# A fused attention and mixer kernel: first pair in parts of two slots, five additive pairs, and a new rule for ScalarE's relus

## The chip, the core and the metric

The kernel runs on one core of a Trainium2 chip. The metric is the device time of one execution in microseconds (us), taken as the median of several runs. The core has TensorE (PE in the profile, with PEld for its weight loads), VectorE (DVE), ScalarE (ACT), GpSimd (POOL) and SyncE (SP), each with its own instruction queue that is worked off in order. [...] SP, ACT and POOL can also issue DMAs.

## What is computed

Four batches, eight heads, 768 positions, head dimension 64. Attention is block-sparse: block i of 32 positions sees itself, its neighbours, the first and the last block and three sampled blocks. An MLP-mixer layer follows, first over the tokens, then over the channels:

```python
mask = np.abs(blk_i - blk_j) <= window
mask = mask | (blk_i == 0) | (blk_j == 0) | (blk_i == n_blocks - 1) | (blk_j == n_blocks - 1)
for qb in range(n_blocks):
    for kb in sampled_blocks[qb]:
        mask[qb*block:(qb+1)*block, kb*block:(kb+1)*block] = True
scores = np.where(mask, scale * np.matmul(q, k.transpose(0, 1, 3, 2)), -1e9)
attn   = softmax(scores)
x      = (attn @ v), heads side by side               # (4, 768, 512)
h      = np.maximum(x^T @ w_tok1, 0.0) @ w_tok2
u      = x + h^T
out    = u + np.maximum(u @ w_ch1, 0.0) @ w_ch2
```

## The kernel before

Two heads make a pair; there are 16 pairs, four to a batch. A pair has nine steps: 3 blocks of 256 queries (t) times 3 blocks of 256 keys (jj). One step is four score matmuls into a PSUM tile `ps` (two such tiles exist), one `exp` of 128x1024 on ScalarE into `et`, and eight value matmuls (`po`). After three steps VectorE divides by the row sums and writes `x`. So a step has one exp and 12 matmuls.

The mask is applied in one of two ways. In the first `NT0` = 4 pairs it is additive: 24 more rows lie under the 64 rows of q and k (`R` = rows 64 to 87, one per block of 32), with an indicator of the key's block on the k side and the entries of `t2add` (0 or -30000) on the q side, so that the score matmul adds the mask itself. It then has 88 rows, and each head has its own buffer columns. From pair 4 on the two heads lie in rows 0 to 63 and 64 to 127, and VectorE multiplies each `et` by a 0/1 `mask` (L709). That mask is spread by GpSimd out of a small one while the first pairs run.

Keys and queries arrive with positions in rows and are turned on TensorE (pairs 1 to 7) or by the DMA's transpose (pairs 8 to 15). Additive pairs take the turn straight from the loaded tile and are evacuated one head at a time (L662); the others are laid out again on VectorE first (L570).

The mixer's work for batch 0 is done per pair in small pieces (`tok_first`: L913, L936, L945, L959, L971). Only when all four of these are done can `ch`, the channel part (L994 for `w_ch1`, L1020 for `w_ch2`), run in earnest. From there on `ch` fills TensorE between attention steps, since it needs no exp.

The order on every engine is written by `Planner`: a small clock with a price for each operation picks, whenever an engine is free, the ready operation of highest priority; streams are `qk_stream`, `pv_stream`, the turns, the token parts and `ch`. The planner's order is what the chip then works off; its prices only decide that order. A relu of `ch` may go to VectorE or ScalarE (`relu_op`, L819 and L821). ScalarE takes one only while no score tile waits for its exp (`exp_pending`).

The first pair is written by hand ahead of the planner. Its q and k come as fp32 in halves of three slots (a slot is 128 positions). ACT issues the first half of q, SP the sampled blocks, both halves of k, then the second half of q. They are cast (L392), turned (L400) and evacuated (L408). GpSimd makes the indicator `ind` with two `affine_select`s over 24x768 (L331, L335), then the identity (L339), and then issues the loads: v of pair 0, k, q and v of pairs 1 and 2, the token weights, pair 3 (L259, L267). VectorE makes `t2add` in fourteen small operations (L358 to L380). `e2_mm` (L415) multiplies `t2add` with the indicator to make the q-side rows for 384 queries, and `e2_copy` (L422) puts them into `qtb`. Meanwhile `idle_mm` (L321) keeps TensorE running. The planner starts at a set time `START`.

Of the kernel before, what the change touches and what calls it, by code (L numbers as in the profile page):

```python
# [10 lines left out]
I32 = mybir.dt.int32  # L11
# [39 lines left out]
class Planner:  # L51
# [8 lines left out]
    PE_LAT, SEM = 180.0, 50.0  # L60
    tight = 40e3
# [42 lines left out]
    def step(self):  # L104
# [31 lines left out]
        for eng in ("act", "dve", "sp"):  # L136
# [3 lines left out]
            best = None  # L140
            for o in self.ops:
                prio, num, engines, cost, deps, emit, done, lat, tags = o
                if eng not in engines:
                    continue
                if eng == "act" and prio > 0 and self.exp_pending:
                    continue
                t = self.when(deps, tags)
                if t is None:
                    continue
                if t <= self.now:  # L150
                    if best is None or (prio, num) < best[:2]:
                        best = o
                else:
                    nxt.append(t)
# [20 lines left out]
def kernel(  # L175
# [24 lines left out]
    NT0 = 4  # L200
    TOKP = 0.7
# [23 lines left out]
    dma = {"free": 7.95 * US, "n": 0}  # L225
    RATE = 200.0
    LATE = (0, 290, 350, 0, 0, 190, 40, 700, 0)
# [8 lines left out]
    def flat(ap):  # L236
# [4 lines left out]
        for n in range(NR)  # L241
# [3 lines left out]
    homes[4]["v"] = flat(ktb[0][:, 1, :])  # L245
    homes.append({"k": flat(qtb[0][:, 1, :]), "q": flat(ktb[1][:, 1, :]), "v": flat(qtb[1][:, 1, :])})
    homes.append({"k": flat(ktb[2][:, 1, :]), "q": flat(qtb[2][:, 1, :]), "v": flat(ktb[3][:, 1, :])})
# [4 lines left out]
                  "v": flat(half["q"][:, 0:S])})  # L252

# [51 lines left out]
    first(nc.sync, "k", k, 1)  # L305
# [3 lines left out]
    ind = ktb[0][:, 0, :].rearrange("k (c p) -> k c p", c=NC)  # L309
    kbi = sb1.tile([128, 24], I32, name="kbi")  # L310
# [9 lines left out]
    def idle_mm():  # L320
        nc.tensor.matmul(  # L321
            out=idle_ps[:, 0, :], lhsT=free(one[:, 0:1], 0, [[0, 128]]),
            rhs=free(one[:, 0:1], 0, [[0, 512]]), start=True, stop=True,
        )

    for i in range(8):
        idle_mm()
# [4 lines left out]
        out=ind[R, :, :], in_=free(one[R, 0:1], 0, [[0, NC], [0, 128]]), compare_op=ALU.is_ge,  # L332
        fill=0.0, base=0, pattern=[[1, NC], [NC, 128]], channel_multiplier=-32,
    )
    nc.gpsimd.affine_select(  # L335
        out=ind[R, :, :], in_=ind[R, :, :], compare_op=ALU.is_ge, fill=0.0,
        base=31, pattern=[[-1, NC], [-NC, 128]], channel_multiplier=32,
    )
    nc.gpsimd.affine_select(  # L339
# [3 lines left out]
    load_pair(0, 3.4 * US, 0, ("v",))  # L343
    load_pair(1, 4.2 * US, 1)
# [5 lines left out]
    sampf = sb1.tile([128, 6], FP32, name="sampf")  # L350
    kbf = sb1.tile([128, 24], FP32, name="kbf")
    dkf = sb1.tile([128, 24], FP32, name="dkf")
    edge = sb1.tile([128, 1], FP32, name="edge")
    bandg = sb1.tile([128, 24], FP32, name="bandg")
    allow = sb1.tile([128, 24], FP32, name="allow")
    t2add = sb1.tile([128, 24], BF16, name="t2add")

    nc.vector.tensor_copy(out=dkf[R, :], in_=dki[R, :])  # L358
    nc.vector.tensor_copy(out=edge[R, :], in_=qbi[R, :])
    nc.vector.tensor_tensor(out=dkf[R, :], in0=dkf[R, :], in1=dkf[R, :], op=ALU.mult)  # L360
    nc.vector.tensor_scalar(
        out=edge[R, :], in0=edge[R, :], scalar1=-11.5, scalar2=None, op0=ALU.add
    )
    nc.vector.tensor_tensor(out=edge[R, :], in0=edge[R, :], in1=edge[R, :], op=ALU.mult)
    nc.vector.tensor_scalar(
        out=edge[R, :], in0=edge[R, :], scalar1=121.0, scalar2=None, op0=ALU.is_gt
    )
    nc.vector.tensor_scalar(
        out=bandg[R, :], in0=dkf[R, :], scalar1=1.0, scalar2=edge[R, 0:1],
        op0=ALU.is_le, op1=ALU.max,  # L370
    )
    nc.vector.memset(free(bandg[R, 0:1], 0, [[23, 2]]), 1.0)
    nc.vector.tensor_copy(out=kbf[R, :], in_=kbi[R, :])
    nc.vector.tensor_copy(out=sampf[R, :], in_=samp64[R, :].bitcast(I32))
    for col, other in ((0, bandg), (2, allow), (4, allow)):
        nc.vector.scalar_tensor_tensor(
            out=allow[R, :], in0=kbf[R, :], scalar=sampf[R, col : col + 1], in1=other[R, :],
            op0=ALU.is_equal, op1=ALU.max,
        )
    nc.vector.tensor_scalar(  # L380
        out=t2add[R, :], in0=allow[R, :], scalar1=-MASKVAL, scalar2=MASKVAL,
        op0=ALU.mult, op1=ALU.add,
    )
    indf = ind[R, :, :].rearrange("k c p -> k (c p)")
    nc.vector.tensor_copy(out=ktb[0][R, 1, 0:384], in_=indf[:, 0:384])
    bandrows = free(ind[R, 0, :], 0, [[0, 2], [1, S]])
    for n in range(1, NV):
        nc.sync.dma_start(out=ktb[n][R, :, :], in_=bandrows)


    def first_lay(copy, nm, hf):
        copy(  # L392
            out=lay0[nm][:, 3 * hf : 3 * hf + 3, :, :],
            in_=f32[nm][:, :, 3 * hf : 3 * hf + 3, :].rearrange("p h c d -> p c h d"),
        )

    def first_turn(nm, hf):
        t = psM.tile([128, 3, 128], BF16, tag="pm", name=f"t{nm}first{hf}")
        for c in range(3):
            nc.tensor.matmul(  # L400
                out=t[:, c, :], lhsT=lay0[nm][:, 3 * hf + c, :, :].rearrange("p h d -> p (h d)"),
                rhs=ident[:, :], start=(c == 0), stop=(c == 2), is_transpose=True,
            )
        return t

    def first_evac(copy, nm, hf, hd, t):
        buf = (ktb if nm == "k" else qtb)[0]
        copy(  # L408
            out=buf[0:64, hd, 384 * hf : 384 * hf + 384],
# [3 lines left out]
    def e2_mm(hf, pool, tag):  # L413
        t = pool.tile([128, 512], FP32, tag=tag, name=f"pm_e2_{hf}")
        nc.tensor.matmul(  # L415
            out=t[R, 0:384], lhsT=t2add[R, :], rhs=indf[:, 384 * hf : 384 * hf + 384],
            start=True, stop=True,
        )
        return t

    def e2_copy(copy, hf, hd, t):
        copy(out=qtb[0][R, hd, 384 * hf : 384 * hf + 384], in_=t[R, 0:384])  # L422

    vcopy, acopy = nc.vector.tensor_copy, nc.scalar.copy
    first_lay(acopy, "q", 0)
    qt0 = first_turn("q", 0)
    first_lay(acopy, "k", 0)
    kt0 = first_turn("k", 0)
    e2a, e2b = e2_mm(0, psM, "pm"), e2_mm(0, psO, "po")
    for i in range(4):  # L430
        idle_mm()
    first_evac(acopy, "q", 0, 0, qt0)
    first_evac(acopy, "q", 0, 1, qt0)
    e2_copy(acopy, 0, 0, e2a)
    first_evac(vcopy, "k", 0, 0, kt0)
    first_evac(vcopy, "k", 0, 1, kt0)
    e2_copy(vcopy, 0, 1, e2b)
    first_lay(acopy, "k", 1)
    first_lay(vcopy, "q", 1)
    START = 6.3 * US  # L440
# [3 lines left out]
    P.free_at["dve"] = START + 550.0  # L444
    f_there = {("k", 0): Ev(START), ("q", 0): Ev(START), ("k", 1): Ev(), ("q", 1): Ev()}

# [4 lines left out]
    def first_rest():  # L451

        def band(eng):
            nc.vector.tensor_copy(out=ktb[0][R, 1, 384:S], in_=indf[:, 384:S])

        P.op(("dve",), {"dve": 250.0}, [], band, prio=0)
        for nm in ("k", "q"):
            box, last, rel = {}, Ev(), Ev()

            def emit(nm=nm, box=box, rel=rel):  # L460
                P.take("pm", rel)
                box["t"] = first_turn(nm, 1)

            yield 330.0, [Ev(START + (200.0 if nm == "k" else 600.0))], [("pm", 1)], emit, last
            for hd in range(2):
                def evac(eng, nm=nm, hd=hd, box=box):
                    first_evac(vcopy, nm, 1, hd, box["t"])

                ev = P.op(("dve",), {"dve": 350.0}, [last], evac, prio=0)
                f_there[nm, 1].same_as = ev  # L470
                rel.same_as = ev
        box, last, rel = {}, Ev(), Ev()

        def emit():
            P.take("pm", rel)
            box["t"] = e2_mm(1, psM, "pm")

        yield 330.0, [], [("pm", 1)], emit, last
        for hd in range(2):
            def copy(eng, hd=hd, box=box):  # L480
                e2_copy(vcopy, 1, hd, box["t"])

            e2_there = P.op(("dve",), {"dve": 555.0}, [last], copy, prio=0)
            rel.same_as = e2_there
        rows_there[0] = e2_there
        built.add(("row", 0))
        for n in range(1, NV):
            def spread(eng, n=n):
# [6 lines left out]
                ("dve",) if n == 1 else ("sp",), {"dve": 560.0, "sp": 800.0}, [e2_there], spread,  # L495
# [104 lines left out]
    def transposes(p):  # L600
# [4 lines left out]
        if p == 0:  # L605
# [3 lines left out]
            for hd in range(2):  # L609
                kT_there[p, hd], qT_there[p, hd] = f_there["k", 1], f_there["q", 1]  # L610
# [108 lines left out]
    def qk_deps(p, t, jj):  # L719
# [3 lines left out]
        deps = [f_there["k", int(jj > 0)], f_there["q", int(t > 0)]]  # L723
        return deps + [rows_there[0]] * (t > 0)

    def qk_stream():
        todo = list(steps)
        while todo:
# [13 lines left out]
            s2 = todo.pop(0)  # L742
            yield lambda p=s2[0]: (p, 1) in qT_there
            evs = [Ev(), Ev()], [Ev(), Ev()]

            def emit(s=s, s2=s2, evs=evs):
                scores(s, evs[0][0], evs[1][0])
                scores(s2, evs[0][1], evs[1][1])
# [410 lines left out]
```

## Time and profile before

| | us |
|---|---|
| median of 9 runs | 255.72 |
| lowest, highest | 255.0, 258.23 |
| the profiled execution | 255.03 |
| its span in the trace | 253.3 |
| PE busy in the span | 245.3 |
| DVE busy | 179.5 |
| ACT busy, of it 144 exps | 174.4, of it 139.1 |

Two of the nine runs lie at 258; the other seven between 255.0 and 255.81. The profiled execution is 1.7 us longer than its span. A row of instructions in the profile gives line, engine, operation, output<-input, shapes and count, then busy time and the mean duration of one in ns, then the engine's idle time before them and what ended it. A timeline row gives start, duration, the same names, and in brackets the idle time before it. A matmul's duration includes its pipeline's latency, so the distance between starts, not the duration, is what it costs TensorE.

### The profile page before, as it was taken

The page shows a single profiled execution, that of the slowest core. Times are in us where ns is not written, and L with a number is a line of the kernel's source. Part 1 is how long each engine was busy: PE and PEld are TensorE (multiplying, and loading weights), DVE is VectorE, ACT ScalarE, POOL GpSimd, SP SyncE. Part 2 cuts the span into 40 slices and gives each one's busy share as a digit, 9 for nine tenths or more (in the row PEclk, how much of TensorE's full clock was granted, in tenths as well). Part 3 has the DMA queues.
Part 4 walks back from the last instruction along what each step waited for, and adds up shares of the span by engine and source line. Part 5 has one row for each costly group of instructions (what it writes and reads, how often), then busy time and mean ns, then how long its engine had stood idle before and what let it go on. Part 6 is the DMA issues. An engine that isn't in the chain of part 4 may idle for free.

```text
span 253.3 us, 6660 instructions
## 1 busy us (share of the span) xinstructions
PE 245.3 (97%) x2786; PEld 159.7 (63%) x2805; DVE 179.5 (71%) x394; ACT 174.4 (69%) x216; POOL 49.9 (20%) x84
## 2 busy tenths in 40 slices
PE   8889999999999999999999999999999999999995
PEld 3679999756666456656676566567567644566444
DVE  7884878998898988899889898978985312200222
ACT  5899999888888577778888777677786510277000
POOL 8846979477300000000000000000000000000000
PEclk9999999999999999999999999999999999999999
DMA  5999999999955935254032212311400212300132
GB/s 145 191 215 202 211 203 205 204 201 201 201 89 126 155 90 95 40 136 103 3 77 51 62 44 46 102 44 44 104 3 1 55 51 84 124 3 0 41 115 94
DMA packets 42462, 26.36 MB, mean 104 GB/s; under 512 B 23680, under 2 KB 38800, under 8 KB 42432
## 3 DMA queue, kind: packets, MB, share of 16 engines
q0 software_dynamic: 15104, 12.98, 32.3%
q1 hardware_dynamic: 27056, 12.76, 20.5%
q8 instruction: 22, 0.36, 0.6%
q10 hardware_dynamic: 272, 0.20, 0.3%
q14 instruction: 8, 0.07, 0.1%
HBM read 26.74 MB, written 6.29 MB: 130 GB/s over the span
## 4 chain that ended last, share of the span: by engine, by line
PE 90%; ACT 4%; DVE 3%; issue 1%
PE pm_ch L994 25%; PE pm_ch L1020 24%; PE ps L691 16%; PE po L777 14%; ACT et L701 3%; PE pm_tok L882 3%; PE pm_tok L857 3%; PE ps_idle L321 2%; PE pm_tok L913 1%; DVE et L709 1%; PE pm_tok L936 1%; PE tk L633 1%; DVE qtb L422 0%; DVE qtb L662 0%; PE tq L633 0%
## 5 line engine op out<-in xcount | busy, mean ns | idle before, releaser
L701 ACT ACTIVATE et<-ps 128x1024 bf16<-128x1024 f32 x144 | 139.1, 1022 | 31.8 <-PE ps L691 30.9
L994 PE MATMUL pm_ch<-uT,w_ch 128*128 128x384 bf16 x384 | 72.6, 326 | 0.1
L709 DVE TENSOR_TENSOR et<-et,mask 128x1024 bf16<-128x1024 bf16 x108 | 70.3, 682 | 1.2 <-ACT et L701 1.2
L1020 PE MATMUL pm_ch<-w_ch,rc 128*128 128x512 bf16 (+2 forms) x293 | 67.8, 362 | 1.1 <-issue 0.3
L777 PEld LDWEIGHTS <-et 128*128 128x128 bf16 x1152 | 47.6, 97 | 16.6 <-issue 3.4
L691 PE MATMUL ps<-qtb,ktb 64*128 64x256 bf16 (+1 forms) x576 | 54.6, 272 | 2.4 <-ACT et L701 2.1
L777 PE MATMUL po<-vaug,et 128*128 128x65 bf16 x1152 | 54.3, 193 | 0.3 <-DVE et L709 0.2
L994 PEld LDWEIGHTS <-w_ch 128*128 128x128 bf16 x384 | 34.3, 97 | 20.7 <-issue 2.7
L1032 DVE TENSOR_TENSOR o<-pm_ch,x 128x512 f32<-128x512 f32 x23 | 15.8, 687 | 41.5 <-PE pm_ch L1020 41.5
L819 ACT ACTIVATE rc<-pm_ch 128x384 bf16<-128x384 f32 x58 | 28.5, 492 | 24.2 <-PE pm_ch L994 24.1
L691 PEld LDWEIGHTS <-ktb 64*128 64x128 bf16 (+1 forms) x576 | 29.0, 95 | 21.7 <-issue 16.7
L1020 PEld LDWEIGHTS <-rc 128*128 128x128 bf16 x312 | 27.3, 98 | 24.4 <-issue 1.9
L821 DVE TENSOR_SCALAR rc<-pm_ch 128x384 bf16<-128x384 f32 x38 | 21.1, 555 | 6.9 <-PE pm_ch L994 6.4
L792 DVE TENSOR_TENSOR x<-po,recip 128x256 bf16<-128x256 f32 x48 | 20.4, 424 | 1.7
L791 DVE RECIPROCAL recip<-po 128x4 f32<-128x4 f32 x48 | 8.6, 179 | 10.2 <-PE po L777 9.9
L890 DVE TENSOR_TENSOR x<-pm_tok,x 128x512 bf16<-128x512 f32 x18 | 11.8, 683 | 2.4 <-PE pm_tok L882 2.4
L882 PE MATMUL pm_tok<-a_t,w_tok 128*128 128x256 bf16 x72 | 10.0, 275 | 0.0
L857 PE MATMUL pm_tok<-x,w_tok 128*128 128x256 bf16 x72 | 9.2, 273 | 0.0
L882 PEld LDWEIGHTS <-w_tok 128*128 128x128 bf16 x72 | 7.5, 127 | 0.6 <-issue 0.2
L259 POOL DMA_DIRECT2D vraw<-in_v_dram x10 | 7.4, 738 | 2.3 <-DVE x L792 1.0
L537 POOL COPY mask<-maskb 128x240 bf16<-128x240 bf16 (+1 forms) x18 | 7.8, 506 | 0.0
L259 POOL DMA_DIRECT2D kraw<-in_k_dram x9 | 6.7, 747 | 4.7 <-DMA w_tok<-in_moe_w_tok_dram 2.2
(104 smaller groups left out, 133.5 us busy)
## 6 DMA issues: line engine op xcount, KB each, us to landing
out_dram<-o SPq DMA_DIRECT2D x23, 256.0 KB, 2.0
w_ch<-in_moe_w_ch_dram POOLq DMA_DIRECT2D x8, 384.0 KB, 10.0
vraw<-in_v_dram POOLq DMA_DIRECT2D x10, 192.0 KB, 7.4
kraw<-in_k_dram POOLq DMA_DIRECT2D x9, 192.0 KB, 8.1
qraw<-in_q_dram POOLq DMA_DIRECT2D x9, 192.0 KB, 7.3
w_tok<-in_moe_w_tok_dram POOLq DMA_DIRECT2D x2, 384.0 KB, 10.0
ktb<-in_v_dram POOLq DMA_DIRECT2D x3, 192.0 KB, 7.4
kf<-in_k_dram SPq DMA_DIRECT2D x2, 192.0 KB, 3.2
```

The costliest lines, as they stand in the source:

```text
L691: nc.tensor.matmul(out=ps[:, hd, 256 * i : 256 * i + 256], lhsT=ktb[n][rows, h, 256 * jj + 128 * i : 256 * jj + 128 * i + 128], rhs=qtb[n] ...
L701: nc.scalar.activation(out=et[:, :, :], in_=ps[:, :, :], func=AF.Exp, scale=0.125)
L709: nc.vector.tensor_tensor(out=ets[s][:, :, :].rearrange("k h (i q) -> k h i q", i=2), in0=ets[s][:, :, :].rearrange("k h (i q) -> k h i q" ...
L777: nc.tensor.matmul(out=po[:, hd, c, :], lhsT=et[:, hd, 256 * i + 128 * c : 256 * i + 128 * c + 128], rhs=va[:, hd, 2 * jj + i, 0:65], star ...
L792: nc.vector.tensor_tensor(out=free(xs[b][:, pb // 2, 2 * t, 128 * (pb % 2) : 128 * (pb % 2) + 128], 0, [[64, 2], [256, 2], [1, 64]],), in0 ...
L819: nc.scalar.activation(out=o(), in_=i, func=AF.Relu)
L821: nc.vector.tensor_scalar(out=o(), in0=i, scalar1=0.0, scalar2=None, op0=ALU.max)
L857: nc.tensor.matmul(out=box["pm"][:, t, :], lhsT=w_tok1[:, sc, 128 * t : 128 * t + 128], rhs=xs[b][:, g, sc, :], start=(t == 0 and sc == 0) ...
L882: nc.tensor.matmul(out=ubox["pm"][:, i, :], lhsT=w_tok2[:, t, :, 2 * s2 + i], rhs=a_t[:, t, :], start=(i == 0 and t == 0), stop=(i == 1 an ...
L994: nc.tensor.matmul(out=pbox["pm"][:, 0:384], lhsT=w_ch1[:, dmc, 128 * cc : 128 * cc + 128], rhs=st[b]["uT"][:, dmc // 2, 3 * sh : 3 * sh + ...
L1020: nc.tensor.matmul(out=pbox["pm"][:, 0:n], lhsT=box["rc"][:, cc, 128 * sc : 128 * sc + 128], rhs=w_ch2[:, cc, lo : lo + n], start=(cc == 0 ...
L1032: nc.vector.tensor_tensor(out=o[:, :].rearrange("p (g e) -> p g e", g=2), in0=pbox["pm"][:, :].rearrange("p (g e) -> p g e", g=2), in1=st[ ...
```

## The change

- **First pair.** q goes in thirds (two slots), k as two slots and then four. The cast of k is all on ScalarE. The second half of k is issued from ACT's queue, right behind the first half of q, and no longer from SP's. The score step waits, block by block, for the thirds of q and of the mask rows (`q_first`, `e2_first`). One `e2_copy` of 24x2x256 serves both heads. `START` is 5.75 us where it was 6.3.
- **Loads.** The indicator is made in two parts with `ident` ahead of both; v of pair 0 and k of pair 1 are issued between the two parts, q and v of pair 1 after the second.
- **The mask's rows** are computed in nine VectorE operations instead of fourteen, three of them TENSOR_TENSOR (before: two, and three SCALAR_TENSOR_TENSOR; after: one of these).
- **Pair 4** is additive: `NT0` = 5. The number of masked steps falls to 99 and is odd, so the first masked step is visited alone.
- **ScalarE** may take a relu while an exp is outstanding, if by the planner's clock the relu ends before that exp can start.
- **Priorities and waits.** `TOKP` goes from 0.7 to 1.5; the first pair's rest has a stream of priority 0.3; the first `ch` group of a row waits for the last turn of `tok_first(3)` (`turned`). The planner's arrival times of loads and the places where later loads land (`homes`, `until`) change too.

```diff
-                if eng == "act" and prio > 0 and self.exp_pending:
+                if eng == "act" and prio > 0 and self.now + cost["act"] > exp_at + self.GRACE:
                     continue
...
-    NT0 = 4
-    TOKP = 0.7
+    NT0 = 5
+    TOKP = 1.5
...
     first(nc.scalar, "q", q, 0)
     first(nc.sync, "k", k, 0)
-    first(nc.sync, "k", k, 1)
+    first(nc.scalar, "k", k, 1)
     first(nc.sync, "q", q, 1)
...
+    def ind_part(lo, n):
+        part = ind[R, lo : lo + n, :]
+        nc.gpsimd.affine_select(
+            out=part, in_=free(one[R, 0:1], 0, [[0, n], [0, 128]]), compare_op=ALU.is_ge,
+            fill=0.0, base=lo, pattern=[[1, n], [NC, 128]], channel_multiplier=-32,
+        )
+        nc.gpsimd.affine_select(
+            out=part, in_=part, compare_op=ALU.is_ge, fill=0.0,
+            base=31 - lo, pattern=[[-1, n], [-NC, 128]], channel_multiplier=32,
+        )
...
-    load_pair(0, 3.4 * US, 0, ("v",))
-    load_pair(1, 4.2 * US, 1)
+    ind_part(0, 2)
+    load_pair(0, 2.4 * US, 0, ("v",))
+    load_pair(1, 3.2 * US, 1, ("k",))
+    ind_part(2, 4)
+    load_pair(1, 5.2 * US, 1, ("q", "v"))
     load_pair(2, 6.4 * US, 2)
...
+    for res, val, lo, hi, op in (
+        (notband, dki, -1.0, 1.0, ALU.not_equal), (inner, qbi, 1.0, 22.0, ALU.is_equal),
+    ):
+        nc.vector.tensor_scalar(
+            out=res[R, :], in0=val[R, :], scalar1=lo, scalar2=hi, op0=ALU.max, op1=ALU.min
+        )
+        nc.vector.tensor_tensor(out=res[R, :], in0=val[R, :], in1=res[R, :], op=op)
...
+    for i in range(7):
+        idle_mm()
+    first_lay(acopy, "q", 0, 2)
+    qt0 = first_turn("q", 0, 2)
+    idle_mm()
+    e2a = e2_mm(0, psO, "po")
+    first_lay(acopy, "k", 0, 2)
+    kt0 = first_turn("k", 0, 2)
+    first_lay(acopy, "k", 2, 4)
+    for i in range(2):
+        idle_mm()
+    kt1 = first_turn("k", 2, 4)
+    idle_mm()
+    for hd in range(2):
+        first_evac(vcopy, "q", 0, 2, hd, qt0)
+    e2_copy(acopy, 0, e2a)
+    for hd in range(2):
+        first_evac(vcopy, "k", 0, 2, hd, kt0)
+    nc.vector.tensor_copy(out=ktb[0][R, 1, 256:S], in_=indf[:, 256:S])
+    for hd in range(2):
+        first_evac(vcopy, "k", 2, 4, hd, kt1)
...
-            s2 = todo.pop(0)
-            yield lambda p=s2[0]: (p, 1) in qT_there
...
+            visit = [s]
+            if s != (NT0, 0, 0) or len(todo) % 2:
+                visit.append(todo.pop(0))
...
+                    deps = [st[b]["uT_there"][dmc], ch1_there[dmc]]
+                    if b == 0 and first:
+                        deps.append(turned)
...
+    P.stream(0.3, transposes(0))
```

## The prediction

> **What bounds the kernel now.** I read the page's busy rows and slices first, then the windows of PE and ACT by stage, then ACT's timeline and the chain of waits in the first 50 us.
>
> ```profile
> PE 245.3 (97%) x2786; PEld 159.7 (63%) x2805; DVE 179.5 (71%) x394; ACT 174.4 (69%) x216; POOL 49.9 (20%) x84
> ...
> PE   8889999999999999999999999999999999999995
> ...
> ACT  5899999888888577778888777677786510277000
> ```
>
> PE is full nearly everywhere; ACT is full only in slices 3 to 7. So the end is set by when PE gets work and how much. The windows (us, then busy us and count of PE, PEld, DVE, ACT, POOL; clock, DMA share, GB/s):
>
> ```profile
> 6.45:18.85 12.40, 10.40 (x155) 8.40 (x154) 10.40 (x27) 11.24 (x13) 8.01 (x12) 1.00 1.21 204
> 18.85:43.20 24.35, 24.14 (x402) 22.54 (x401) 18.15 (x45) 23.84 (x26) 20.49 (x37) 1.00 1.23 205
> ...
> 37.00:51.30 14.30, 13.73 (x246) 11.83 (x243) 13.15 (x31) 12.58 (x14) 10.29 (x18) 1.00 1.27 204
> 51.30:194.20 142.90, 141.80 (x1744) 89.17 (x1759) 126.35 (x264) 111.92 (x132) 11.34 (x16) 1.00 0.47 89
> ```
>
> Until 18.85 PE loses 2 us. From there to 43 both PE and ACT are full. From 51.3, where `ch` (L994) begins in earnest, PE loses only 1.1 us in 143, and the chain of waits is all PE. Hence: **the time is the moment at which `ch` begins, plus the PE work left then.** Before that moment ACT's exps set the pace, since a step cannot be pushed through faster than one exp:
>
> ```profile
> 7.09 1.02 ACT L701 ACTIVATE et<-ps 128x1024 bf16<-128x1024 f32 x1
> 8.49 7.97 ACT L701 ACTIVATE et<-ps 128x1024 bf16<-128x1024 f32 x8 [0.38 <-PE ps L691]
> 16.95 0.80 ACT L662 COPY ktb<-tk 64x768 bf16<-64x768 bf16 x1 [0.49 <-DVE ktb L662]
> 17.77 10.56 ACT L701 ACTIVATE et<-ps 128x1024 bf16<-128x1024 f32 x11
> ```
>
> An exp starts every 0.953 us (ten from 17.77 to 27.30). ACT loses 0.38 behind the first exp and 1.3 between pairs 0 and 1 (16.46 to 17.77). The chain of waits names the second loss: VectorE evacuates pair 1's q late, and ScalarE does a copy for pair 2 in front of the exp:
>
> ```profile
> 14.88 0.42 DVE x L792
> 15.31 0.46 DVE qtb L662
> 15.77 0.01 issue
> 15.78 0.56 DVE qtb L662
> 16.34 0.03 issue
> 16.37 0.56 DVE ktb L662
> 16.93 0.02 issue
> 16.95 0.80 ACT ktb L662
> 17.76 0.02 issue
> 17.77 1.03 ACT et L701
> ```
>
> From 44 on ACT has gaps (0.69, 0.80, 0.42 us): pair 4 is masked, and VectorE is the chain from 46.96 to 51.25 with three masks of `et`, a q evacuation and the last `tok_first`. Only 42 exps are done by 51.8.
>
> **First pair.** POOL: the two 24x768 selects took 0.86 each, the 128-column one 0.29; a line through both gives 0.40 for 256 columns and 0.63 for 512. POOL then ends `ident` at 1.6 and the first part at 2.5, issues v0 at 2.6 and k1 at 3.5 (before 3.39 and 4.26), makes the second part until 5.6, and issues q1 at 5.6 (before 4.97), v1, k2 and all later loads some 0.65 later than before.
>
> VectorE's two 24x24 TENSOR_TENSORs took 0.86 and 0.80 and end 0.03 behind the two selects, so they sat them out. With selects of 0.29 and 0.40 there they end near 1.6 and 2.1. `t2add` ends near 3.8, against 4.98.
>
> ACT: cast of q at 3.46 as now (its DMA), 0.51 x 2/3 = 0.35, cast of k0 to 4.2, cast of k1, 0.52, `e2_copy` 0.55. The two behind k0 wait for k1's landing, and ACT's exps queue behind them: **this is the wait that the change adds.** The trace has k0 landing 2.6 us after its issue and k1 and the second q 3.7. k1's issue moves from 1.78 to 1.24, so it lands between 3.9 and 4.9. The Trainium skill ("DMA: Bandwidth & Descriptors", "Issuing engines are not separate DMA queues") speaks against a gain: another issuing engine saves only issue time, since the 16 DMA engines are shared. By it k1 comes 0.54 earlier and no more, at 5.0; by the row of k0, which had no `ktb<-ktb` copies beside it (these now start after 5.6), at 3.9. I take 4.5. ACT's table load (1.28 us) begins 0.45 later and ends at 3.0, under q's landing. Then `e2_copy` ends at 5.6, VectorE's evacuations of q and k0 (four of 0.28) too, the first score runs at 5.7 (before 6.45) and the first exp at 6.35 (before 7.09). The second needs the band copy (0.3) and two k evacuations (0.44 each): 6.8, no gap. The fourth exp needs the second third of q. DVE must do `e2_copy` (0.69), cast (0.3), v's copy (0.36, v0 issued 0.8 sooner), cast (0.3) and two evacuations (0.28 each), so 9.0; score 9.05, exp at **9.7**, between 9.4 (no gap) and 10.4. Before, it was 8.49 + 2 x 0.953 = 10.4. Gain 0.7.
>
> **Between pairs 0 and 1.** The built program turns all of pair 1's k and q on PE before score step seven of pair 0, and all copies of pairs 1 and 2 are on VectorE, ahead of ACT's need by more than 1 us. The 1.3 us go. What is late next is q1: its turn stands in PE's queue ahead of step seven and should start at 11.3; issued at 5.6 with the shortest landing of its group, 6.0, it comes at 11.6. I charge 0.3 (0 to 1.7, the group's median being 7.7).
>
> **Pair 4 additive.** Nine more exps run without masks: nine of 0.68 us and two layouts of 0.35 leave VectorE. PE pays. Eight 64-row scores of two steps take 0.54; four 88-row ones take 0.44. The Trainium skill ("TensorEngine Tiling (Array Packing)", "Theoretical Speedup") puts row tiling of at most 64 rows at up to twice the speed: 0.44 against 0.22 a step, so giving it up would cost 9 x 0.22 = 2.0 us. By the row it is 9 x (0.44 - 0.27) = 1.5, and I take the row. It lies before `ch`, in time that the exps set anyway.
>
> **When `ch` begins.** The built program places it behind the values of pair 4's last step, the 45th exp, with step 46 scored and all of `tok_first` done. The fourth exp at 9.7, 42 x 0.953 = 40.0 to the end of the 45th, 0.3 for q1, 0.3 for values and latency: 50.3. PE must keep up: from 9.9 on 41 scores (0.44), 43 steps of values (0.245), 72 turns (0.056), 96 token matmuls (0.056), 24 turns of u and the small mask (1.6) are 18.0 + 10.5 + 4.0 + 5.4 + 1.6 = 39.5 us in 40.4: 98%, as full as the window from 18.85 to 43.2 where it kept up (99%). I add 0.2: **50.5**, 0.8 before 51.3.
>
> **What is left then.** In the chain of the masked stretch scores are 0.195 and values 0.196 of 143 us, so 0.27 each a step. Before, at 51.3, 42 steps were scored, 39 valued, all turns on PE done, and three `ch` matmuls. After: 46, 45, 12 turns undone, no `ch`. Left over: -4 x 0.27 - 6 x 0.27 + 12 x 0.056 + 3 x 0.163 = **-1.5 us**.
>
> **ScalarE's relus.** By the built order 23 relus of `ch` stand ahead of the last exp on ACT (before 20), 26 beside the masks on VectorE (before 37). PE idles 1.1 us in that stretch at most to be won. The planner's price is 415 ns; rows give 492. If each of 23 delays an exp by the 77 ns, that is 1.8 us, nearly all behind PE's other work (ACT is 78% busy there). I take 0, from -0.5 to +1. `turned`, `TOKP` and the new homes only change the order already counted, and the lone masked visit is one step.
>
> **Sum.** -0.8 - 1.5 = -2.3 us on the profiled 255.03, so 252.7. The seven close runs lie mostly at 255.7, 0.7 above it; from the median 255.72 - 2.3 = **253.4**.
>
> **Rivals.**
> - *The front gives nothing and PE falls behind.* For it: PE at 98% with its order fixed, the 2 us it lost before 18.85, and k1 and v0 as waits in ACT's and DVE's queues. Against: 24 us in which both engines ran full. Fourth exp at 10.4, 2% of 40 us lost: `ch` begins at 52.0, 0.7 - 1.5 = -0.8: 254.9. Chance 0.19.
> - *A late load, slower.* q1 stands behind two selects on POOL, and every later PE instruction stands behind its turn. With the group's longest landing, 10.2, it comes at 15.8, 4.5 after its turn's place, and -2.3 - 0.3 + 4.5 = +1.9: 257.6. It decides from a landing of 8.3 us after the issue. For it: the median of 7.7 is near. Against: queues are short that early. Chance 0.10.
> - *More than I counted.* Relieved of masks and relus VectorE lets PE close its 1.1 us, and the front gives all 1.0: 252.0. Chance 0.10.
> - That the ScalarE rule does nothing costs no more than 0.5 and sits in the range.
>
> **Numbers.** The forecast has 0.61, with 252.5 to 254.4 of its own. Two runs of this kernel that differ by under 0.5% (1.28 us) can't be told from no change. Faster by more (below 254.44): nearly all of the forecast's, the 0.10, and a third of the first rival's: 0.77. Within: 0.14. Slower: 0.09. Eight in ten: 252.1 to 255.7.
>
> **What would show it.** ACT's timeline: first exp before 6.6, fourth near 9.7, tenth near 15.7 with no copy before it, 45 exps in a row with no relu and no gap over 0.4. The chain from 46 to 51 without VectorE's masks. `ch` from 50.5 on. It is wrong if k1 lands after 5.5, if PE waits for q1, if PE shows waits between 20 and 50, or if PE loses more than 2 us between 51 and the last values.

## The result

| | before | changed |
|---|---|---|
| median | 255.25 us (31 runs) | 254.05 us (10 runs) |
| ratio, 95% interval | | 0.9946 (0.9925 to 0.9966) |
| profiled execution, its span | 255.03, 253.3 | 254.14, 252.4 |

The change makes the kernel 0.5% faster, 1.2 us by the medians and 0.9 us by the two profiled executions, where 2.3 us were forecast. 254.05 lies inside the forecast range and 0.65 above the forecast itself. But the 31 runs of the kernel before, the nine that the forecast started from among them, have a median of 255.25, not 255.72. So the error in the gain is 1.1 us: about half of the forecast gain came. By the medians it is also a little less than the 1.28 us that the prediction named as the least that can be told from no change. The interval of the ratio, 0.9 to 1.9 us faster, does lie clear of it.

The page's busy row and slices of the changed kernel:

```profile
PE 246.2 (98%) x2786; PEld 162.1 (64%) x2804; DVE 168.4 (67%) x374; ACT 177.6 (70%) x224; POOL 49.8 (20%) x86
...
PE   8999999999999999999999999999999999999994
...
ACT  5899999998888878678989797677665710277000
```

The span less PE's busy time gives the balance: PE stands idle for 252.4 - 246.2 = 6.2 us, before 253.3 - 245.3 = 8.0. Its idle time shrank by 1.8 us, and it is busy for 0.9 us more. VectorE is 11 us less busy; how much of that reaches the time, its row does not say.

The windows that were shown of before, now of the changed kernel (columns as there):

```profile
6.45:18.85 12.40, 11.71 (x166) 9.08 (x166) 11.84 (x28) 11.40 (x13) 8.93 (x13) 1.00 1.17 193
18.85:43.20 24.35, 24.28 (x435) 22.94 (x432) 16.31 (x43) 23.99 (x27) 20.31 (x37) 1.00 1.23 205
37.00:51.30 14.30, 14.23 (x257) 13.16 (x254) 9.46 (x26) 14.03 (x16) 10.00 (x18) 1.00 1.27 204
51.30:194.20 142.90, 141.79 (x1719) 90.80 (x1731) 121.51 (x254) 112.63 (x137) 11.06 (x16) 1.00 0.47 89
```

PE's loss up to 18.85 went from 2.0 to 0.7, that from 37 to 51.3 from 0.57 to 0.07. The long stretch behind shows 1.1 in both kernels, but that is no wait. Some matmuls are missing from both traces, as the page of the changed kernel shows, and below it that of e11, one of the runs that follow:

```profile
L1047 PE MATMUL pm_ch<-w_ch,rc 128*128 128x512 bf16 (+2 forms) x294 | 67.3, 362 | 0.9 <-issue 0.2
L1047 PEld LDWEIGHTS <-rc 128*128 128x128 bf16 x312 | 27.5, 98 | 24.6 <-issue 1.5
...
L1047 PE MATMUL pm_ch<-w_ch,rc 128*128 128x512 bf16 (+2 forms) x312 | 70.4, 363 | 0.0
```

There are 312 weight loads and 294 matmuls (before: 312 and 293). The traces of e9 to e12 have all 312, and in them PE is idle for 0.04 us or less between 51.5 and 185, where both kernels here show 1.1. So TensorE had nothing to gain there. Both traces lack about the same, so their difference stands.

ACT's timeline of the changed kernel:

```profile
6.58 3.05 ACT L717 ACTIVATE et<-ps 128x1024 bf16<-128x1024 f32 x3 [0.69 <-PE ps L707]
10.30 25.92 ACT L717 ACTIVATE et<-ps 128x1024 bf16<-128x1024 f32 x27 [0.68 <-PE ps L707]
36.55 8.56 ACT L717 ACTIVATE et<-ps 128x1024 bf16<-128x1024 f32 x9 [0.32 <-ACT et L717]
45.28 6.82 ACT L717 ACTIVATE et<-ps 128x1024 bf16<-128x1024 f32 x7 [0.17 <-PE ps L707]
52.36 0.49 ACT L839 ACTIVATE rc<-pm_ch 128x384 bf16<-128x384 f32 x1 [0.26 <-PE pm_ch L1018]
```

46 exps follow each other with no copy and no relu between. The loss of 1.3 us between pairs 0 and 1 is gone: the tenth exp lies inside the row that begins at 10.30. But that row begins at 10.30, not 9.7, and the exps lose 0.32 and 0.17 later. The channel part begins at 51.67, not 50.5. The chain of waits up to that point, and the line with which it begins before:

```profile
48.90 0.73 PE po L797 x24
49.63 0.44 PE ps L707 x4
50.07 0.11 PE tk L649 x2
50.18 0.22 PE tq L649 x4
50.40 0.33 PE ps L707 x4
50.73 0.59 PE po L797 x16
51.32 0.11 PE tq L649 x2
51.43 0.24 PE po L797 x8
51.67 0.49 PE pm_ch L1018 x3
...
51.29 0.49 PE pm_ch L994 x2
```

VectorE's masks, which were the chain from 46.96 to 51.25, have left it. What is on it now is TensorE itself, without a gap. What comes after is as reckoned: a late point that both kernels share, a long row of the second channel matmuls (`w_ch2`), begins at 202.34 where it began at 203.25:

```profile
203.25 15.70 PE L1020 MATMUL pm_ch<-w_ch,rc 128*128 128x512 bf16 x70
...
202.34 15.70 PE L1047 MATMUL pm_ch<-w_ch,rc 128*128 128x512 bf16 x70
```

The channel part began 0.38 later and this point came 0.91 sooner, so 1.3 us less work was left, where 1.5 were reckoned.

### The profile page after: what moved, and what is told of

Same layout as the page of the kernel before. It is cut to its first block, busy times and chain, and to the rows that moved or that the text cites. A ratio compares the mean times of both kernels' runs of the same rounds, so it can differ in the third digit from the quotient of the medians.

```text
span 252.4 us, 6647 instructions
## 1 busy us (share of the span) xinstructions
PE 246.2 (98%) x2786; PEld 162.1 (64%) x2804; DVE 168.4 (67%) x374; ACT 177.6 (70%) x224; POOL 49.8 (20%) x86
## 4 chain that ended last, share of the span: by engine, by line
PE 93%; ACT 3%; DVE 1%; issue 1%
PE pm_ch L1018 25%; PE pm_ch L1047 24%; PE ps L707 17%; PE po L797 14%; PE pm_tok L902 3%; ACT et L717 3%; PE pm_tok L877 3%; PE ps_idle L328 1%; PE pm_tok L958 1%; PE tk L649 1%; PE pm_tok L935 1%; PE tq L649 1%; DVE ktb L411 0%; PE pm_ut L981 0%; DVE qtb L425 0%
## 5 line engine op out<-in xcount | busy, mean ns | idle before, releaser
L1018 PE MATMUL pm_ch<-uT,w_ch 128*128 128x384 bf16 x384 | 71.8, 326 | 0.0
L725 DVE TENSOR_TENSOR et<-et,mask 128x1024 bf16<-128x1024 bf16 x99 | 63.8, 683 | 1.7 <-ACT et L717 1.7
L797 PEld LDWEIGHTS <-et 128*128 128x128 bf16 x1152 | 49.1, 97 | 15.9 <-issue 3.0
L707 PE MATMUL ps<-qtb,ktb 64*128 64x256 bf16 (+1 forms) x576 | 57.7, 272 | 0.8 <-ACT et L717 0.3
L797 PE MATMUL po<-vaug,et 128*128 128x65 bf16 x1152 | 55.7, 193 | 0.2 <-PE ps L707 0.2
L839 ACT ACTIVATE rc<-pm_ch 128x384 bf16<-128x384 f32 x70 | 34.1, 493 | 26.3 <-PE pm_ch L1018 26.1
L707 PEld LDWEIGHTS <-ktb 64*128 64x128 bf16 (+1 forms) x576 | 30.7, 95 | 16.6 <-issue 12.4
L841 DVE TENSOR_SCALAR rc<-pm_ch 128x384 bf16<-128x384 f32 x26 | 14.4, 553 | 3.0 <-PE pm_ch L1018 2.7
L902 PE MATMUL pm_tok<-a_t,w_tok 128*128 128x256 bf16 x72 | 10.7, 276 | 0.0
L902 PEld LDWEIGHTS <-w_tok 128*128 128x128 bf16 x72 | 7.6, 128 | 1.7 <-issue 1.1
L877 PEld LDWEIGHTS <-w_tok 128*128 128x128 bf16 x72 | 6.4, 98 | 1.7 <-issue 0.8
```

Of the source, the lines that this page charges most:

```text
L707: nc.tensor.matmul(out=ps[:, hd, 256 * i : 256 * i + 256], lhsT=ktb[n][rows, h, 256 * jj + 128 * i : 256 * jj + 128 * i + 128], rhs=qtb[n] ...
L725: nc.vector.tensor_tensor(out=ets[s][:, :, :].rearrange("k h (i q) -> k h i q", i=2), in0=ets[s][:, :, :].rearrange("k h (i q) -> k h i q" ...
L797: nc.tensor.matmul(out=po[:, hd, c, :], lhsT=et[:, hd, 256 * i + 128 * c : 256 * i + 128 * c + 128], rhs=va[:, hd, 2 * jj + i, 0:65], star ...
L839: nc.scalar.activation(out=o(), in_=i, func=AF.Relu)
L841: nc.vector.tensor_scalar(out=o(), in0=i, scalar1=0.0, scalar2=None, op0=ALU.max)
L877: nc.tensor.matmul(out=box["pm"][:, t, :], lhsT=w_tok1[:, sc, 128 * t : 128 * t + 128], rhs=xs[b][:, g, sc, :], start=(t == 0 and sc == 0) ...
```

## The experiments

Two theories. **A** is the prediction's: up to the channel part the exps set the pace, TensorE has room, and what the additive pair costs it there is hidden. **B**: TensorE is full from some 10 us on, so its work and its idle time are the time, and the additive pair is paid for. All kernels were timed beside the kernel before; a ratio is to that kernel. Its median was 255.24 beside e1 to e4, 255.46 beside e5 to e8 and 255.26 beside e9 to e12, so a difference of 0.2 us between two of these groups means nothing by itself.

| run | median, us | ratio, 95% interval |
|---|---|---|
| e5, the changed kernel again | 254.11 | 0.9934 (0.9906 to 0.9961) |
| e1, pair 4 masked | 254.66 | 0.9960 (0.9942 to 0.9979) |
| e2, new first pair alone | 254.51 | 0.9959 (0.9941 to 0.9976) |
| e3, all but the first pair | 255.83 | 1.0006 (0.9980 to 1.0033) |
| e4, q's cast on ScalarE, new plan | 255.06 | 0.9978 (0.9956 to 0.9999) |
| e6, the same in the old order | 253.59 | 0.9920 (0.9894 to 0.9946) |
| e7, v0 and k1 issued later | 254.21 | 0.9940 (0.9916 to 0.9965) |
| e8, old relu rule | 254.08 | 0.9941 (0.9923 to 0.9959) |
| e9, 18 more matmuls | 255.83 | 1.0028 (1.0017 to 1.0038) |
| e10, nine more copies on ScalarE | 255.16 | 0.9991 (0.9970 to 1.0012) |
| e11, second half of k from SP | 254.14 | 0.9959 (0.9946 to 0.9971) |
| e12, old priority, no wait | 254.67 | 0.9978 (0.9970 to 0.9987) |

**The changed kernel once more**, as the measure for the rows below it.

> The changed kernel itself, beside the three that follow, so that they are compared in the same session: 253.9 to 254.4 us.

254.11. The ten runs of the changed kernel had come in two groups, 253.92 to 254.14 and 254.34 to 254.51. The profiled execution here was of the upper kind (254.54), and ACT's timeline shows what went with it:

```profile
4.88 0.92 ACT L395 CAST klay_first<-kf 128x256 bf16<-128x256 f32 x2 [1.07 <-DMA kf<-in_k_dram]
...
10.87 25.77 ACT L717 ACTIVATE et<-ps 128x1024 bf16<-128x1024 f32 x27 [0.50 <-PE ps L707]
```

The cast of k waits for the first half of k until 4.88; in the first profile it began at 4.32. The fourth exp follows with the same delay, 10.87 against 10.30. Of the runs below, e7's trace has the late cast (5.04) and 254.52, e8's the early one (4.37) and 254.03. Four executions agree; that makes the link to the two groups of times likely, not shown.

**The two halves of the change.**

```diff
# e2: the changed kernel, with
-    NT0 = 5
-    TOKP = 1.5
+    NT0 = 4
+    TOKP = 0.7
-                if eng == "act" and prio > 0 and self.now + cost["act"] > exp_at + self.GRACE:
+                if eng == "act" and prio > 0 and self.exp_pending:
-                    if b == 0 and first:
-                        deps.append(turned)
# and the old homes.  e3: the kernel before, with all of these new, and its own first pair and loads
```

> The new first pair, its loads and its stream alone; four additive pairs, the old rule for ScalarE, the old priority and homes. Theory A: the loss between pairs 0 and 1 goes (1.3 us) and the fourth exp comes 0.1 sooner, 1.0 to 1.4 us faster than before, and VectorE's masks stay on the chain near 50 us. Theory B: the same or more, 1.3 to 2.0 us, since TensorE's losses before 18.85 go and no additive work is added. If most of the gain came from pair 4, it is under 0.5 us.

> The first pair as before; five additive pairs, the new rule for ScalarE, the priority, the wait for the last turn and the homes. Theory A: exps from 17.77 us on without a gap, 45th ends near 52.3, channel part near 52.7 with 6 more steps scored and valued: 1.0 us faster than before. Theory B: TensorE pays 1.4 us for the additive pair and saves 0.6: 0.3 to 0.8 us slower than before.

The new first pair alone gives 0.7 us by the medians, less than either theory; by its interval it is 0.6 to 1.5, which leaves room for A. In its chain of waits VectorE is the chain from 43.5 to 50.06, as it was before the change near 50 us: the earlier exps run into it. The rest alone is not faster, which is against A's 1.0 us. By the medians it is 0.6 us slower, as B had it, but its interval, from 0.5 faster to 0.8 slower, contains no change as well. Its windows:

```profile
6.45:18.85 12.40, 10.50 (x155) 8.55 (x154) 10.51 (x27) 11.13 (x13) 8.38 (x12) 1.00 1.22 209
18.85:43.20 24.35, 24.18 (x417) 22.70 (x417) 15.55 (x41) 24.21 (x27) 19.94 (x37) 1.00 1.23 205
```

PE's early loss of 1.9 us is still there, so is the copy on ScalarE between pairs 0 and 1 (at 17.07), and behind them a full PE has more to do. So by the medians the two halves do not add: -0.7 and +0.6 alone, -1.2 together. The chains would explain it: the first pair clears VectorE's and PE's losses ahead, and the additive pair takes VectorE off the chain that the earlier exps would meet. That is argued, not shown: the intervals are wide enough for halves that add. The planner also made a new order for each of e1, e2, e3, e8 and e12, and by e4 and e6 below a new order alone can cost 1.5 us.

**Pair 4 masked again.**

```diff
-    NT0 = 5
+    NT0 = 4
```

> The changed kernel with four additive pairs instead of five, nothing else. Theory A (the prediction's: ScalarE's exps set the pace until the channel part begins, and nine more exps without masks cost TensorE nothing there): it loses what pair 4 gave, about +1 us against the changed kernel, so near the time before. Theory B (TensorE is full from 9.7 us on in the changed kernel, so its work is the time; the additive pair costs it 9 x 0.15 to 0.17 = 1.4 us and only saves the 0.6 us that it lost between 37 and 51 us): 0.4 to 1.4 us faster than the changed kernel, 252.7 to 253.6.

254.66: 0.6 us slower than the changed kernel by the medians, on A's side of it (+1), where B had it 0.4 to 1.4 faster. That B is excluded: the fastest of its 22 runs took 254.37. The profiled span is 252.4, as long as the changed kernel's; PE is 0.6 us less busy (245.6) and waits 0.6 more. The chain of waits shows where:

```profile
40.59 0.42 DVE x L812
41.02 0.94 DVE x L967 x2
...
43.44 0.36 DVE x L812
43.80 0.54 DVE uT L995
```

With masks on it, VectorE is late with the token pieces. The additive pair trades this for TensorE time, at par in the profile. So neither theory has it right. Of the 0.6 us by the medians 0.4 lie outside the span: 2.1 us in e1's runs, 1.7 in the changed kernel's. I have no cause for that; it stays open.

**More work for one engine at a time.**

```diff
# e9: the first score matmul of a step of pairs 2 and 3 issued twice
+                reps = 2 if p in (2, 3) and i == 0 and hd == 0 else 1
+                for again in range(reps):
...
# e10: ahead of each exp of pair 2
+            if p == 2:
+                nc.scalar.copy(out=spare[:, :], in_=ident[:, :])
```

> The changed kernel with the first score matmul of each step of pairs 2 and 3 issued twice: 18 matmuls of 256 columns more, 18 x 0.109 = 2.0 us of TensorE between 20 and 41 us, every order unchanged, the result unchanged. Theory A (exps set the pace there, TensorE has the 2 % of 40 us that the prediction left it): 1.2 us or less slower than the changed kernel. Theory B (TensorE is full): 1.8 to 2.0 us slower, 255.9 to 256.1.

> The changed kernel with a copy of 128x128 on ScalarE ahead of each exp of pair 2: nine, some 0.2 us each, 1.8 us of ScalarE between 27 and 36 us, every order unchanged, the result unchanged. Theory A: the exps set the pace, so nearly all of it, 1.5 to 1.8 us slower than the changed kernel. Theory B alone (TensorE full, ScalarE only nearly so): part of it is hidden, under 1.3 us. With e9 it tells which engine is the bound there, or that both are.

Against the 254.1 of the changed kernel e9 costs 1.7 of 2.0 us. In e10 each copy takes 0.19 of ScalarE ahead of its exp:

```profile
24.74 0.29 ACT L719 COPY spare<-ident 128x128 bf16<-128x128 bf16 x1
24.93 1.03 ACT L720 ACTIVATE et<-ps 128x1024 bf16<-128x1024 f32 x1
25.84 0.30 ACT L719 COPY spare<-ident 128x128 bf16<-128x128 bf16 x1
```

Nine of them are 1.7 us, and 1.1 us arrive at the end. The changed kernel was not timed beside these two; by the ratios, against its 0.9946, e9 costs 2.1 and e10 1.1, each uncertain by some 0.6 to 0.8. So each engine is the bound for part of the way. A's room of 0.8 us for TensorE is hardly there, and e10's 1.1 is B's side (under 1.3), though A's 1.5 is not excluded.

The traces say how much ScalarE can hide. In e10 the nine exps with copies start every 1.10 us, and the same nine of the changed kernel (23.72 to 32.33) every 0.957: nine times 0.146 is 1.3, so 0.4 of the 1.7 us fell into time in which ScalarE had waited. Its own pace is read where the chain of waits runs through the exps alone, here in the changed kernel:

```profile
14.19 0.80 ACT et L717
15.00 0.10 issue
15.10 0.82 ACT et L717
15.91 0.09 issue
16.00 0.90 ACT et L717
```

Exps then start 0.90 to 0.91 us apart, and in e10 the copy starts 0.91 behind the exp ahead of it (24.93 to 25.84). The prediction's 0.953 is slower than that: it is a mean over ten exps from 17.77 to 27.30 of the kernel before, and from 18.85 to 30.05 that kernel's chain is TensorE's:

```profile
29.54 0.44 PE ps L691 x4
29.98 0.07 PE pm_tok L913
30.05 0.03 issue
30.08 0.94 ACT et L701
```

So the 0.953 already held TensorE's share. In the changed kernel the 42 steps from the fourth exp (10.30) to the 46th (51.08) take 40.8 us, 0.971 each; at ScalarE's own 0.905 they would take 38.0; in its chain ScalarE is the bound from 14.19 to 17.97 and from 32.32 to 37.6, and TensorE for the rest between 10 and 51.67.

**The front of the kernel.** Four runs move one thing each and keep the order of everything else, but for e4. In e4 the planner makes a new order, and its price for the other cast of q is 530 ns where it was 300.

```diff
# e6 (e4 is the same, with the planner making a new order of it)
     e2_copy(acopy, 0, e2a)
+    first_lay(acopy, "q", 2, 2)
-                lambda eng, t=t: first_lay(vcopy, "q", 2 * t, 2), prio=0,
+                lambda eng, t=t: t == 2 and first_lay(vcopy, "q", 4, 2), prio=0,
# e7
+    ind_part(2, 4)
     load_pair(0, 2.4 * US, 0, ("v",))
     load_pair(1, 3.2 * US, 1, ("k",))
-    ind_part(2, 4)
# e11
-    first(nc.scalar, "k", k, 1)
+    first(nc.sync, "k", k, 1)
```

> The changed kernel with the cast of q's second third on ScalarE, in its 0.69 us gap before the first exp, instead of on VectorE (0.53 us in front of the fourth exp's score). Theory A: the fourth exp starts at 9.5 to 9.8 instead of 10.30 and everything behind it with it: 0.5 to 0.7 us faster than the changed kernel. Theory B: TensorE gets its work only as far sooner as its own waits at 7.9 to 9.7 shrink: 0.3 to 0.6 us. If that gap is hidden by what follows: no difference.

> As e4, the cast of q's second third on ScalarE before the first exp, but with every other instruction in the changed kernel's order on every engine (e4's planner had rearranged TensorE's and VectorE's queues). Theory A and B agree here: VectorE is 0.5 us sooner at the evacuation, the fourth exp starts at 9.8 to 9.9 instead of 10.30 and the channel part 0.3 to 0.5 sooner, 0.2 to 0.5 us faster than the changed kernel; e4's loss was then its new order. If this is not faster, what comes after 10 us hides the first pair's last gap, and the prediction's 9.7 for the fourth exp was not the term that cost it.

> The changed kernel with both parts of the indicator ahead of v of pair 0 and k of pair 1 on GpSimd, the order on all other engines unchanged: v0 is issued near 3.9 instead of 2.48, q1 no later. Theory A: VectorE's copy of v0, which stands ahead of the fourth exp's last evacuations, waits 0.3 to 0.8 us longer, so the kernel is 0.3 to 0.6 us slower than the changed one. If the sooner issue is worth nothing: no difference.

> The changed kernel with the second half of k issued from SP again, behind the first, so near 1.78 us instead of 1.27; nothing else moves. By the trace of the changed kernel the first half landed later than before (cast at 4.32 instead of 3.96) with the second half beside it on the other queue. If issue order is what counts, the first half's cast comes at 3.9 to 4.0, the second half's not before 5.0, and the first exp 0.2 to 0.6 us later: up to 0.4 us slower. If only the sum of the bytes counts: no difference within 0.2 us.

e4 was a miss: 0.95 us slower than the changed kernel. ACT's timeline shows its fourth exp near 10.0 as hoped, but gaps of 0.46, 0.48 and 0.59 at 16, 42 and 47 us: told of a cast less on VectorE and a dearer one, the planner had shuffled its own and TensorE's queues for the next 50 us. e6 holds the order fixed and gets what was expected: 253.59, 0.5 us faster than the changed kernel beside it (e5) and the fastest of all that ran. The intervals of the two ratios overlap, but the fastest runs, 253.41 and 253.95, are as far apart. VectorE's timeline, first of the changed kernel, then of e6:

```profile
7.12 0.69 DVE L425 CAST qtb<-pm_e 24x512 bf16<-24x512 f32 x1
7.84 0.53 DVE L395 CAST qlay_first<-qf 128x256 bf16<-128x256 f32 x1
8.29 0.34 DVE L583 COPY vaug<-vraw 128x768 bf16<-128x768 bf16 x1
8.55 0.53 DVE L395 CAST qlay_first<-qf 128x256 bf16<-128x256 f32 x1
9.12 0.61 DVE L411 COPY qtb<-tqfirst 64x256 bf16<-64x256 bf16 x2
```

```profile
7.12 0.69 DVE L425 CAST qtb<-pm_e 24x512 bf16<-24x512 f32 x1
7.84 0.59 DVE L584 COPY vaug<-vraw 128x768 bf16<-128x768 bf16 x1
8.36 0.27 DVE L395 CAST qlay_first<-qf 128x256 bf16<-128x256 f32 x1
8.66 0.61 DVE L411 COPY qtb<-tqfirst 64x256 bf16<-64x256 bf16 x2
```

The evacuation that the fourth exp needs begins at 8.66 instead of 9.12, the exp at 9.85 instead of 10.30, and by the medians the 0.45 us arrive.

e7 makes no difference by its median (254.21 against 254.11): v of pair 0 is issued at 3.79 instead of 2.48 and VectorE's copy of it, at 9.00, still does not wait. (In that profile the first half of k is cast only at 5.04, which puts off the exps by itself.) So that sooner issue is worth nothing that can be measured. e11 is the stranger one. Its ACT timeline:

```profile
3.98 0.41 ACT L395 CAST klay_first<-kf 128x256 bf16<-128x256 f32 x1
5.98 0.62 ACT L395 CAST klay_first<-kf 128x512 bf16<-128x512 f32 x1 [1.59 <-DMA kf<-in_k_dram]
...
7.88 2.85 ACT L717 ACTIVATE et<-ps 128x1024 bf16<-128x1024 f32 x3 [0.69 <-PE ps L707]
11.04 34.31 ACT L717 ACTIVATE et<-ps 128x1024 bf16<-128x1024 f32 x36 [0.31 <-PE ps L707]
```

The second half of k is cast 1.3 us later than with ACT's queue (4.7), the first exp is 1.3 late and the fourth 0.74, yet the median of five runs is 254.14, the changed kernel's. By the timelines the channel part begins only 0.26 later (51.77 for 51.51). From 11.04 on 36 exps run without a gap of the kind that the changed kernel has at 36 us (0.32). So two thirds of a lead of the exps were worth nothing here. In e5's trace, where the fourth exp is 0.57 late, 0.42 of it does arrive (51.93), so how much a lead is worth stays open. e6's lead came with VectorE's queue freed, and there TensorE too got its work sooner (175 matmuls up to 18.85 us, 166 in the changed kernel).

**The relu rule and the priorities.**

```diff
# e8
-                if eng == "act" and prio > 0 and self.now + cost["act"] > exp_at + self.GRACE:
+                if eng == "act" and prio > 0 and self.exp_pending:
# e12
-    TOKP = 1.5
+    TOKP = 0.7
-                    if b == 0 and first:
-                        deps.append(turned)
```

> The changed kernel with the old rule for ScalarE (no relu while an exp is outstanding); the planner makes its order anew. Prediction: the rule is worth 0 (-0.5 to +1 us). Theory B: TensorE is full either way, so 253.7 to 254.6; slower by more than 0.5 us only if VectorE's relus come onto the chain.

> The changed kernel with the old priority of the first token pieces and without the wait of the first channel groups for the last turn; the planner makes its order anew. The prediction counted these at nothing: no difference within 0.4 us, unless the new order takes back turns of pair 1 or 2 late.

e8: 254.08, no difference. Eleven operations fewer run on ScalarE (213 for 224) and eleven more on VectorE; the rule does nothing for the time. e12: 254.67, 0.6 slower, outside what I had expected. Its ACT timeline loses 0.39 at 36 us and then 0.26 and 0.15 between 49 and 52.6, where token pieces that the changed kernel has done by 46.5 now stand between the values. Which of its two edits does it, or only the new order, was not tried.

## Why the prediction was right, and where its size was off

The direction and the parts are right. That the number fell into its range is in part luck: the gain is 1.2 us for 2.3, and by gain (0.8) and start of the channel part (52.0, measured 51.67) the first rival lies nearer than the forecast (50.5).

Right, each by the traces:

- The 1.3 us between pairs 0 and 1 go, and pair 1's turn of q starts at 11.95 with no wait for its load. The 0.3 that I charged were not needed.
- The masks leave the chain between 47 and 51.
- The work left behind the start of the channel part shrinks, by 1.3 us for 1.5.
- The relu rule is worth nothing (e8). The 1.1 us that PE seemed to idle in the long masked stretch, which the third rival wanted to close, are missing records.
- k's second half is cast at some 4.7 (reckoned 4.5), the first exp starts at 6.58 (6.35). Of rule and row at that place neither was the whole. The Trainium skill ("DMA: Bandwidth & Descriptors", "Issuing engines are not separate DMA queues") leaves only the time of the issue, 0.5 us; measured, the second half is cast 1.3 us sooner than in e11, and the measurement decides. But the first half comes later: its cast starts at 4.26 to 5.04 in the eleven traces with the second half on ACT's queue, at 3.93 to 3.98 in the three with both on SP's. That fits the page's other half, that all queues share the same engines. The net effect on the time is nil (e11).

Off by size, in the one sum that set when the channel part begins: 9.7 + 40.0 + 0.3 + 0.3 + 0.2 = 50.5 reckoned (fourth exp, 42 exps, q1, values, TensorE), 10.3 + 40.8 + 0.6 = 51.7 measured (fourth exp, 42 exps, values).

- **The fourth exp, 9.7 reckoned, 10.30 measured.** The k evacuations ended at 7.09 for 6.8, and I priced VectorE's casts of q's thirds at 0.3 each, though the trace's only row for such a cast, of 128x384, had 0.55. They took 0.53 each. Two stood ahead, so 0.46, with the 0.3 before more than the 0.6; the exp came sooner behind its evacuation than reckoned, 0.57 for 0.7. e6 takes one of them away and gets 0.45 back.
- **"It lies before `ch`, in time that the exps set anyway", with 0.2 us for a TensorE at 98%.** There was next to no such time. The step that did not hold is the reading that the exps alone set the pace: TensorE and ScalarE take turns as the bound. The 0.953 us for an exp was a pace that TensorE had part in, and in the changed kernel, with the additive pair's work on TensorE, it was 0.971: 0.8 us over 42 exps. e9 shows that TensorE had next to no room (1.7 of 2.0), e3 that the additive pair alone is no clear gain, e1 that in the profile it is a trade at par.

The priority and the wait are worth 0.6 together with the order that came of them (e12). The prediction counted them inside the built order, so this is no term that it missed.

The first rival was a front for nothing and a TensorE that falls behind. Its two reasons are the two above, at smaller sizes. The late load did not happen.

## What to carry to other kernels

Where two engines are both over 97% busy (from 18.85 to 43.2 us here), ask what each edit does to the work of *both*; a step that is moved under the one is paid on the other. Add a known amount of work to each in turn: the share that arrives at the end is worth more than the busy rows. A mean pace taken where both ran full belongs to neither: find each one's own pace where the chain of waits runs through it alone. Count the records before an idle time is believed. And when an order is planned by prices, test an edit with the order held fixed first, since a new plan can cost more than the edit brings (e4 and e6).

## What was not expected of the hardware

- The same operation on VectorE took up to twice as long at one place as at another: the cast of 128x256 fp32 to bf16 0.53 us at 7.84 and 8.55, but 0.27 at 8.36 in e6; the copy of v 0.59 at 7.84 in e6, but 0.34 at 8.29. A GpSimd DMA issue that begins meanwhile (8.23 and 8.94) suggests itself. For the casts it half fits: over all traces the five into which no such beginning falls took 0.27 to 0.29, the seventeen others 0.29 to 0.54. The copies of v contradict it: in the changed kernel one at 14.43 took 0.59 with no beginning in it, before one at 9.96 took 0.36 with one at 10.11. The cause stays open.
- The time outside the span was 2.0 to 2.1 us in all runs of e1 and 1.65 to 1.8 in those of the other kernels.
